# Pooled attention and a mixer in float32r pairs: low parts of the first four heads and a clamp go to GpSimd, seven more unread products, a new order

## The chip, the cores and the metric

The kernel runs on one core of one Trainium2 chip. The metric is the device time of one execution in microseconds (us); lower is better. Engines are named as in the profile: PE (TensorE, matrix products), ACT (ScalarE), DVE (VectorE), POOL (GpSimd) and SP (SyncE, which issues the DMA transfers).

## The reference

```python
# attention: B=4, H=8 heads, S=1152 keys, D=64
q_pool = q.reshape(B, H, S // 2, 2, D).mean(axis=3)          # 576 queries
scores = (1 / sqrt(D)) * q_pool @ k.transpose(0, 1, 3, 2)
attn = exp(scores - max(scores)); attn /= attn.sum(-1) + 1e-9
x = (attn @ v) as (B, 576, H * D)                            # 512 channels
# mixer: tokens, then channels; the weights are float64 words
u = x + (relu(x.T @ w_tok1) @ w_tok2).T                      # 576 -> 256 -> 576
out = u + relu(u @ w_ch1) @ w_ch2                            # 512 -> 1536 -> 512
```

## The kernel before, in words

Every matrix product runs on float32r operands, and precision is kept by splitting a float32 into a high part (rounded to float32r by a copy) and a low part (the value minus its high part). A product is then made of two or three: high by high, and the ones with a low part.

**Stage one** goes over 32 heads (4 batches of 8). A head has nine steps, each over two units of 128 keys by 288 queries. In a step PE makes the scores into a PSUM tile `s` (line 770); ACT exponentiates it twice, once as float32 into `pf` (line 780) and once rounded into `ph` (line 783); the low part `pl = pf - ph` is made by DVE or POOL (line 787); and PE multiplies `ph` and `pl` by the values `vv` into `o` (line 812). Four `pl` and five `ph` buffers go round. Beside the steps PE makes row maxima of the next head (line 706), which DVE reduces out of three PSUM banks `r` (line 708); keys and queries of the next pair of heads are turned on PE (lines 567, 590) and split; a head ends with products that turn its result (line 834), a reciprocal (line 848) and a scaled copy into `u` (line 853). The heads of `IN_PV` (0 to 3 and the odd ones from 5) get their sums of weights from an extra product; in the others DVE sums `pf` (line 794).

**The token mixer** runs after every fourth head of a half batch, first on heads 0 to 3; on PE it is placed between the products of later heads (lines 887 and 905). Its weights are loaded as 64-bit words and narrowed to float32 in `tok_weights`, in nine groups of columns, each by a chain: an absolute value on ACT (line 351), a clamp (line 352), a mask and shift (line 355), two merges (lines 358 and 361) on DVE, a high part on ACT (line 513) and a low part on DVE or POOL (line 515). Two buffers `w` go round. **Stage two**, the channel mixer (lines 1002 to 1049), follows the last head; its weights are narrowed in the same way, by DVE alone.

The order of the work is made ahead of the run by `Plan.run`: every step has an engine, a cost in ns and a due time. The planner keeps a clock for each engine and takes the step that can start first, ties going to the earlier due time. The due times are the head's start plus an offset out of the table `DUE`. A step made with `both(...)` goes to POOL or to DVE, whichever the planner's clocks let end it first, unless `on` names one. Each engine then runs its instructions in that order, with no regard to what is late on the chip.

Some products are read by nobody: `turn_over` multiplies a tile of `vv` into `o` (line 713). `WARM` of them open the program, and one follows each of the first maxima.

Of the kernel before, what the change touches and what calls it, by code (L numbers as in the profile page):

```python
# [14 lines left out]
ALU = mybir.AluOpType  # L15
# [7 lines left out]
PE, ACT, DVE, POOL, DMA, HOST = range(6)  # L23
# [11 lines left out]
    "p_lo": 0.02,  # L35
    "sum": -2.82,
    "pv": 1.78,
    "o": -107.46,
    "finish": 5.54,
    "max": -22.72,  # L40
    "max_each": 0.53,
    "prep": -32.49,
    "v": 9.58,
    "stack": 29.51,
    "stack_2": 96.51,
# [4 lines left out]
    "sum_each": 1.2,  # L50
    "pv_lo": 0.54,
    "lo_first": 7.78,
    "max_first": -120.52,
    "max_second": 37.69,
    "scores_each": -10.71,
    "p_hi": 0.84,
    "pv_one": -0.04,
    "finish_each": -14.96,
    "den_sum": -47.39,
    "x_lo": 5.05,  # L60
    "x": -54.79,
    "den": -45.22,
    "rd": -27.39,
    "u": 18.75,
    "u_each": 75.19,
    "max_of": 7.22,
    "max_row": -32.02,
    "max_first_each": -127.47,
    "q_pool": -3.78,
    "q_turn": 1.79,  # L70
    "k_each": 1.45,
    "k_hi": -42.28,
    "k_lo": 1.7,
    "q_hi": -79.72,
    "q_lo": 70.53,
    "load_kq": -48.02,
    "load_v": -163.1,
    "v_lo": -10.5,
    "load_w_tok": 117.45,
    "mix_x_lo": 3.96,  # L80
    "mix_1": 3.17,
    "mix_t": 2.11,
    "mix_2": 2.45,
    "mix_u": -79.91,
    "w_ch": 235.24,
    "w_ch_each": -64.39,
    "ut_0": -4.75,
    "ut_1": -50.96,
    "stay": 0.78,
}  # L90


# [145 lines left out]
def kernel(  # L238
# [41 lines left out]
    SP3 = S // 3  # L280
    CM = C // 2
    due = DUE
    WARM = 8
    KEEP = (0, 1, 2, 3)
    UNSTACKED = 1
    IN_PV = (0, 1, 2, 3, *range(5, 32, 2))
    CUT = 3
    FOLDS = 114
    LO = (None,) * 9
    PL = 4  # L290
    PH = 5

# [15 lines left out]
    def act_ps(n):  # L308
        return 50 + 0.833 * n
# [164 lines left out]
    def tok_weights(after):  # L474
# [19 lines left out]
        for i, c, wh, wl in (  # L494
                [(1, c, W1H[:, c], W1L[:, c]) for c in range(NQ)]
                + [(2, c, W2H[:, c], W2L[:, c]) for c in range(NJ)]):
            r = rows(c)
            words_ = (
                staged[:, c * n1:(c + 1) * n1] if i == 1 and c < 4
                else REST if i == 1 else raw[2, c])  # L500
            words_ = words_.rearrange("p (j t) -> p j t", t=2)
            n = words_.shape[1]
            for k, o in enumerate(
                    (slice(0, n),) if n <= 256 else (slice(0, n // 2), slice(n // 2, n))):
                m = o.stop - o.start
# [44 lines left out]
    def prep_kq(p, t):  # L550
# [10 lines left out]
        def keys(j):  # L561
            ps = Buf("s" if p == 0 else "r")
            o = slice(j * SP3, (j + 1) * SP3)

            def turn(ps=ps, j=j):
                for c in range(3):
                    te.transpose(
                        bank(ps)[:, c * P:(c + 1) * P],
                        KN[:, 3 * j + c].rearrange("p h d -> p (h d)"), ident)

            step(PE, 3 * TURN, turn, t + j * due["k_each"], [("kn", 0, j), ("kn", 1, j)],
                 [ps, ("kh", j), ("kl", j)], [ps])
            step(ACT, act_ps(SP3), lambda ps=ps, o=o: sc.copy(KHI[:, o], bank(ps)[:, 0:SP3]),
                 t + j * due["k_each"] + due["k_hi"], [ps], [("kh", j)])
            if p == 0:
                step(POOL, 150 + 1.1 * SP3, lambda o=o: po.tensor_copy(
                    K2[0][0:D, o], KHI[0:D, o]), t, [("kh", j)], [("k2", 0, j)])
            step(DVE, dve(SP3), lambda ps=ps, o=o: ve.tensor_sub(
                KLO[:, o], bank(ps)[:, 0:SP3], f(KHI)[:, o]),
                t + j * due["k_each"] + (due["lo_first"] if p == 0 else due["k_lo"]), [ps, ("kh", j)], [("kl", j)])  # L580
# [168 lines left out]
    def main(h, t0):  # L749
# [8 lines left out]
        for s in range(NS):  # L758
# [3 lines left out]
            for i, (fq, c) in enumerate(units):  # L762
# [23 lines left out]
            pv = h in IN_PV  # L786
            both(2 * HF, lambda e, pf=pf, ph=ph, pl=pl: e.tensor_sub(  # L787
                at(pl), pf, f(at(ph))), t + due["p_lo"], [("pf", s), ph], [pl], [pl],
                on=LO[s])
            if s in (4, NS - 1) and not pv:  # L790
                fq = s // 5
                for y in range(CUT):
# [348 lines left out]
```

## Time and profile before

| | us |
|---|---|
| median of three runs (955.95 to 961.17) | 960.82 |
| the profiled execution, whole | 961.85 |
| its span, from the first to the last instruction | 959.7 |
| PE busy in the span | 921.2 |
| DVE busy | 704.3 |
| ACT busy | 514.7 |
| POOL busy | 341.0 |

The profiled execution's own time is 2.15 us longer than its span. Busy is the time in which an engine had an instruction under way; an instruction that waits for an engine's shared resource after it has begun counts as busy.

### The profile page before, as it was taken

To read this page: it belongs to the slowest core of one execution; us is meant where nothing else is said; L and a number is where in the kernel's file an instruction comes from. 1 tells how busy PE (TensorE), PEld (TensorE's weight loads), DVE (VectorE), ACT (ScalarE), POOL (GpSimd) and SP (SyncE) were. 2 spreads that over 40 slices of the span, in tenths; PEclk is the share of its full clock that TensorE was granted. 3 is DMA by queue.
4 is the path that set the end of the run, shared out by engine and by line. 5 is a ranking of instruction groups with operands and counts; after the bars stand their busy time and mean duration, and the time that the engine had idled before them with its cause. 6 is when DMAs were issued, how large, how long until landed. Compare 5 with 4: busy or idle time off the path is not lost.

```text
span 959.7 us, 15868 instructions
## 1 busy us (share of the span) xinstructions
PE 921.2 (96%) x5850; PEld 841.8 (88%) x5850; DVE 704.3 (73%) x1277; ACT 514.7 (54%) x1040; POOL 341.0 (36%) x308
## 2 busy tenths in 40 slices
PE   6988899999999999999999999999999999999997
PEld 5767788989899898899898998989989999999996
DVE  6888999899999898999989999998882222121211
ACT  3765787776786775786767866854441111111110
POOL 1443386565483563673754844510000000000000
PEclk9978999999999999999999999999999999999999
DMA  6956537536456455365454343024430101000001
GB/s 144 257 113 146 129 79 165 128 80 155 102 128 140 97 124 131 87 155 118 99 131 114 88 99 97 24 90 132 132 110 1 66 1 33 1 33 0 30 4 33
DMA packets 89684, 91.09 MB, mean 95 GB/s; under 512 B 43852, under 2 KB 68808, under 8 KB 89608
## 3 DMA queue, kind: packets, MB, share of 16 engines
q1 hardware_dynamic: 89608, 90.09, 38.7%
q8 instruction: 46, 0.75, 0.3%
q14 instruction: 30, 0.25, 0.1%
HBM read 43.25 MB, written 4.72 MB: 50 GB/s over the span
## 4 chain that ended last, share of the span: by engine, by line
PE 63%; DVE 25%; DMA 5%; issue 3%; ACT 2%; SPq 0%; DVEq 0%; ACTq 0%
PE r L1002 14%; PE o L812 11%; PE s L1030 11%; PE s L770 9%; DVE mx L708 7%; DVE sum L794 6%; PE r L706 6%; PE r L834 3%; DVE pl L787 3%; DMA kk<-kl 2%; DMA raw<-in_moe_w_ch_dram 2%; PE o L1030 2%; PE r L905 2%; PE r L841 2%; PE r L887 1%
## 5 line engine op out<-in xcount | busy, mean ns | idle before, releaser
L787 POOL TENSOR_TENSOR pl<-pf,ph 128x576 fp32r<-128x576 f32 x182 | 260.9, 1454 | 132.1 <-ACT ph L783 93.7
L780 ACT ACTIVATE pf<-s 128x576 f32<-128x576 f32 x288 | 189.5, 662 | 90.9 <-PE s L770 84.9
L708 DVE TENSOR_REDUCE mx<-r 128x1 f32<-128x384 f32 x384 | 197.1, 548 | 15.2 <-PE r L706 12.9
L783 ACT ACTIVATE ph<-s 128x576 fp32r<-128x576 f32 x288 | 189.0, 663 | 3.8 <-PE o L812 2.8
L770 PE MATMUL s<-qq,kk 128*128 128x288 f32 x574 | 168.8, 306 | 2.2 <-ACT ph L783 1.8
L770 PE MATMUL s<-q,k 65*128 65x288 f32 x576 | 165.6, 300 | 0.0
L1010 DVE SCALAR_TENSOR_TENSOR h<-r,h 128x384 fp32r<-128x384 f32 x72 | 40.1, 557 | 169.5 <-ACT h L1008 169.4
L794 DVE TENSOR_REDUCE sum<-pf 128x96 f32<-128x864 f32 x84 | 146.1, 1752 | 0.3
L812 PE MATMUL o<-ph,vv 128*128 128x288 f32 x576 | 143.3, 304 | 1.0 <-ACT ot L817 0.9
L706 PE MATMUL r<-kk,qq 128*128 128x384 f32 x372 | 132.2, 374 | 12.6 <-DVE mx L708 6.4
L1008 ACT ACTIVATE h<-r 128x384 fp32r<-128x384 f32 x72 | 35.4, 491 | 200.3 <-PE r L1002 200.3
L812 PE MATMUL o<-pl,vv 128*128 128x288 f32 x576 | 138.7, 299 | 1.6 <-DVE pl L787 1.6
L1030 PE MATMUL s<-w,h 128*128 128x512 f32 x504 | 131.1, 394 | 0.4 <-DVE h L1010 0.4
L770 PEld LDWEIGHTS s<-qq,kk 128*128 128x128 f32 x574 | 110.0, 192 | 7.0 <-ACT ph L783 5.2
L812 PEld LDWEIGHTS o<-ph,vv 128*128 128x128 f32 x576 | 100.9, 191 | 11.4 <-ACT ot L817 3.7
L770 PEld LDWEIGHTS s<-q,k 65*128 65x128 f32 x576 | 110.6, 192 | 0.0
L1002 PE MATMUL r<-big,w 128*128 128x384 f32 x576 | 110.3, 339 | 0.3 <-DVE big L991 0.3
L1030 PEld LDWEIGHTS s<-w,h 128*128 128x128 f32 x504 | 93.4, 188 | 17.2 <-DVE h L1010 0.7
L1002 PEld LDWEIGHTS r<-big,w 128*128 128x128 f32 x576 | 102.7, 189 | 4.3 <-DVE big L991 0.5
L812 PEld LDWEIGHTS o<-pl,vv 128*128 128x128 f32 x576 | 99.6, 190 | 3.6 <-DVE pl L787 2.5
L787 DVE TENSOR_TENSOR pl<-pf,ph 128x576 fp32r<-128x576 f32 x106 | 93.6, 884 | 3.8 <-issue 1.2
L706 PEld LDWEIGHTS r<-kk,qq 128*128 128x128 f32 x372 | 71.2, 196 | 25.4 <-DVE mx L708 12.6
(135 smaller groups left out, 1258.9 us busy)
## 6 DMA issues: line engine op xcount, KB each, us to landing
raw<-in_moe_w_ch_dram SPq DMA_DIRECT2D x24, 512.0 KB, 3.8
kk<-kh SPq DMA_DIRECT2D x32, 288.0 KB, 3.3
kk<-kl SPq DMA_DIRECT2D x32, 288.0 KB
qq<-qh SPq DMA_DIRECT2D x64, 144.0 KB, 3.7
vn<-in_v_dram SPq DMA_DIRECT2D x32, 288.0 KB, 3.5
k<-kk SPq DMA_DIRECT2D x31, 288.0 KB, 5.1
kn<-in_k_dram SPq DMA_DIRECT2D x30, 288.0 KB, 4.3
qn<-in_q_dram SPq DMA_DIRECT2D x32, 256.0 KB, 3.1
```

What stands on the lines that cost most here:

```text
L706: step(PE, mm(SP3), lambda ps=ps, w=w, x=x: te.matmul(at(ps)[:, 0:SP3], w, x, start=True, stop=True), t, read, [ps], [ps])
L708: step(DVE, dve(SP3), lambda ps=ps, m=m: ve.tensor_reduce(m, at(ps)[:, 0:SP3], axis=AX.X, op=ALU.max), t + due["max_of"], [ps], [key])
L770: te.matmul(at(st)[:, i, 0:HF], w[:, c * P:(c + 1) * P], x[:, fq * HF:(fq + 1) * HF], start=(n == 0), stop=(n == len(terms) - 1))
L780: step(ACT, act_ps(2 * HF), lambda pf=pf, st=st: sc.activation(pf, at(st)[:, :, 0:HF], AF.Exp, scale=ESC), t, [(st, 0), (st, 1)], [("pf", s)])
L783: step(ACT, act_ps(2 * HF), lambda ph=ph, st=st: sc.activation(at(ph), at(st)[:, :, 0:HF], AF.Exp, scale=ESC), t + due["p_hi"], [(st, 0), ...
L787: both(2 * HF, lambda e, pf=pf, ph=ph, pl=pl: e.tensor_sub(at(pl), pf, f(at(ph))), t + due["p_lo"], [("pf", s), ph], [pl], [pl], on=LO[s])
L794: step(DVE, 65 + 1.83 * NK * HF // CUT, lambda fq=fq, cs=cs: ve.tensor_reduce(SUM[:, fq, cs], PF[:, fq * NK:(fq + 1) * NK, cs].rearrange(" ...
L812: lambda o=o, x=x, w=w, m=m, i=i, c=c, new=new, end=end: te.matmul(at(o)[0:m], w[:, c], at(x)[:, i], start=new, stop=end),
L1002: te.matmul(at(ps)[:, 0:GT], w[:, c], x[:, c], start=(c == 0 and n == 0), stop=(c == NC4 - 1 and n == 2))
L1008: step(ACT, act_ps(GT), lambda: sc.activation(at(h)[:, 0], at(ps)[:, 0:GT], AF.Relu), t, [ps], [h])
L1010: step(DVE, dve(GT), lambda: ve.scalar_tensor_tensor(out=at(h)[:, 1], in0=at(ps)[:, 0:GT], scalar=0.0, in1=f(at(h))[:, 0], op0=ALU.max, op ...
L1030: te.matmul(at(ps), a[:, x * P:(x + 1) * P], w, start=(fi == 0 and m == 0), stop=(fi == NF - 1 and m == 2))
```

## The change

It does four things. The low parts `pl` of heads 0 to 3 (`EARLY = 4`) are all made by POOL; before, the planner chose. The clamp of the token mixer's words (the second operation of `narrow`, nine times) is made by POOL and not by DVE. Seven more unread products are issued: `WARM` is 11 and not 8, and four follow the first turning of keys. And nearly all offsets in `DUE` have new values, of which two lines are shown; so the planner gives another order throughout. Lines of the changed file are 11 higher around `main`, 8 higher in `keys`, 1 higher in `narrow`.

```diff
-    "w_tok": -27.04,
-    "w_tok_each": 7.34,
+    "w_tok": 1.44,
+    "w_tok_each": 7.64,
...
-    WARM = 8
+    WARM = 11
...
-    LO = (None,) * 9
+
+    EARLY = 4
...
+                def clamp(tmp=tmp):
+                    po.tensor_scalar(
+                        out=tmp(), in0=tmp(), scalar1=F64_LEAST, scalar2=F64_MOST,
+                        op0=ALU.max, op1=ALU.min)
+
                 for n, (eng, cost, fn) in enumerate(narrow(tmp, lambda w=words_[r, o]: w, m)):
+                    if n == 1:
+                        eng, cost, fn = POOL, 150 + 1.1 * m, clamp
                     step(eng, cost, fn, t, read, [w], [w] if n == 0 else [], shared=eng == DVE)
...
             step(PE, 3 * TURN, turn, t + j * due["k_each"], [("kn", 0, j), ("kn", 1, j)],
                  [ps, ("kh", j), ("kl", j)], [ps])
+            if p == 0 and j == 0:
+                for _ in range(4):
+                    turn_over(220, t - 1, plan.steps[-1:])
...
                 at(pl), pf, f(at(ph))), t + due["p_lo"], [("pf", s), ph], [pl], [pl],
-                on=LO[s])
+                on=POOL if h < EARLY else None)
```

Counted over the whole program, DVE has 94 low parts `pl` where it had 106 (POOL 194 and not 182), no clamps of the token words where it had 9, 11 low parts of values `vv` where it had 16, 6 sums `qp` of query pairs where it had 18, 9 low parts of the mixer's input in the form 128x256 where it had 7, and 4 of the four low parts `w2l` where it had 2. By the buffers that the products read, 21 of the 36 low parts of heads 0 to 3 were DVE's before.

On PE at the start of the program (o<-vv are the unread products, s<-ident turns the first queries `qp` and keys `kn`, r<-kh,big the first maxima), before:

```order
L713 MATMUL o<-vv_122 128x512 x8
L590 MATMUL s_77<-ident,qp 128x128 x3
L567 MATMUL s_78<-ident,kn 128x128 x3
L706 MATMUL r_80<-kh,big_72 128x384
L713 MATMUL o<-vv_122 128x512
```

and now:

```order
L724 MATMUL o<-vv_122 128x512 x11
L601 MATMUL s_77<-ident,qp 128x128 x3
L575 MATMUL s_78<-ident,kn 128x128 x3
L724 MATMUL o<-vv_122 128x512 x4
L717 MATMUL r_80<-kh,big_72 128x384
```

Nothing else moved there: three products more stand ahead of the first turn, and four ahead of the first maximum.

On DVE after the keys of the second pair of heads are split (kl, ql are their low parts, w the words of the token weights, rm the maxima of the last rows), before:

```order
L787 TENSOR_TENSOR pl_163<-pf,ph_157 128x576
L787 TENSOR_TENSOR pl_164<-pf,ph_158 128x576
L614 TENSOR_TENSOR ql_120<-r_81,qh_118 128x384
L614 TENSOR_TENSOR ql_120<-r_82,qh_118 128x192
L352 TENSOR_SCALAR w_155<-w_155 128x256
L352 TENSOR_SCALAR w_156<-w_156 128x256
L355 TENSOR_SCALAR w_155<-w_155 128x256
L355 TENSOR_SCALAR w_156<-w_156 128x256
L358 SCALAR_TENSOR_TENSOR w_155<-u_66,w_155 128x256
L358 SCALAR_TENSOR_TENSOR w_156<-u_66,w_156 128x256
```

and now:

```order
L625 TENSOR_TENSOR ql_120<-r_81,qh_118 128x384
L625 TENSOR_TENSOR ql_120<-r_82,qh_118 128x192
L719 TENSOR_REDUCE rm<-r_80 128x1
L719 TENSOR_REDUCE rm<-r_81 128x1
L719 TENSOR_REDUCE rm<-r_82 128x1
L356 TENSOR_SCALAR w_155<-w_155 128x256
L359 SCALAR_TENSOR_TENSOR w_155<-u_66,w_155 128x256
L362 SCALAR_TENSOR_TENSOR w_155<-u_66,w_155 128x256
L641 TENSOR_TENSOR vv_122<-vn,vv_122 128x9x64
L523 TENSOR_TENSOR big_71<-w_155,big_70 128x256
L564 TENSOR_TENSOR qp<-qn 128x256 x2
L857 TENSOR_SCALAR den_130<-r_80 128x5
```

The low parts and the clamps are gone, and one group of words stands here where two stood side by side. Over a longer stretch: up to the reciprocal that ends head 3, DVE had 25 low parts `pl`, all 36 of its operations on token words (four for each of nine groups), 2 `w2l` and 1 `vv`; it now has 3, 17 of 27, none and 4. From there to the reciprocal of head 8 it had 11 `pl`, no words, no `w2l` and 3 `vv`; it now has 17, the other 10, all 4 and 2. From there to the reciprocal of head 31 it had 70 `pl`, 12 `vv`, 13 `qp` (6 in the form 128x256) and 3 low parts of the mixer's input in the form 128x256; it now has 74, 5, none and 5. The first product of the token mixer stands behind the end of head 6 in both orders.

On POOL from its first low part on (vv and v are the values, qp the sums of query pairs), before:

```order
L787 TENSOR_TENSOR pl_163<-pf,ph_158 128x576
L787 TENSOR_TENSOR pl_164<-pf,ph_159 128x576
L630 TENSOR_TENSOR vv_121<-vn,vv_121 128x9x64
L632 COPY v_123<-vv_121 128x9
L634 MEMSET vv_121 128x9
L787 TENSOR_TENSOR pl_162<-pf,ph_161 128x576
L556 TENSOR_TENSOR qp<-qn 128x256
L556 TENSOR_TENSOR qp<-qn 64x128
L787 TENSOR_TENSOR pl_165<-pf,ph_159 128x576
L515 TENSOR_TENSOR big_71<-w_156,big_70 128x256
```

and now:

```order
L798 TENSOR_TENSOR pl_164<-pf,ph_159 128x576
L798 TENSOR_TENSOR pl_165<-pf,ph_160 128x576
L643 COPY v_123<-vv_121 128x9
L645 MEMSET vv_121 128x9
L564 TENSOR_TENSOR qp<-qn 128x256
L564 TENSOR_TENSOR qp<-qn 64x128
L798 TENSOR_TENSOR pl_162<-pf,ph_161 128x576
L798 TENSOR_TENSOR pl_163<-pf,ph_157 128x576
L513 TENSOR_SCALAR w_155<-w_155 128x256
L798 TENSOR_TENSOR pl_164<-pf,ph_158 128x576
L798 TENSOR_TENSOR pl_165<-pf,ph_159 128x576
L798 TENSOR_TENSOR pl_162<-pf,ph_160 128x576
```

The low parts now follow one another, and the first clamp (L513) stands between two of them. From its first low part to the last of head 3 POOL has 36 low parts, 1 `vv`, 4 copies `v`, 4 clears of a column of `vv`, 7 sums `qp` (3 in the form 128x256, 4 in 64x128) and 6 clamps.

## Rows read from the trace of the kernel before

**Rows 1.** Head of the page: busy us, share of the span, instructions.

```profile
PE 921.2 (96%) x5850; PEld 841.8 (88%) x5850; DVE 704.3 (73%) x1277; ACT 514.7 (54%) x1040; POOL 341.0 (36%) x308
```

**Rows 2.** DVE's timeline: reciprocals of heads 0, 1, 3, 8 and 31.

```profile
48.81 0.19 DVE L848 RECIPROCAL rd<-den 128x5 f32<-128x5 f32 x1
84.45 0.18 DVE L848 RECIPROCAL rd<-den 128x5 f32<-128x5 f32 x1
124.14 0.18 DVE L848 RECIPROCAL rd<-den 128x5 f32<-128x5 f32 x1
218.84 0.18 DVE L848 RECIPROCAL rd<-den 128x5 f32<-128x5 f32 x1
632.59 0.18 DVE L848 RECIPROCAL rd<-den 128x5 f32<-128x5 f32 x1
```

**Rows 3.** Windows between those: length; busy us of PE, PEld, DVE, ACT, POOL; PEclk; DMA.

```profile
20.00:48.80 28.80, 24.11 (x152) 20.69 (x151) 22.74 (x49) 21.59 (x46) 12.69 (x13) 0.94 1.08 251
48.80:84.50 35.70, 29.99 (x154) 25.45 (x155) 31.75 (x63) 21.17 (x45) 16.16 (x16) 0.75 0.64 137
84.50:104.20 19.70, 17.78 (x122) 16.07 (x121) 18.05 (x37) 13.50 (x29) 7.19 (x9) 0.94 0.39 91
104.20:124.10 19.90, 17.92 (x125) 16.02 (x124) 17.19 (x35) 12.84 (x25) 5.63 (x6) 1.00 0.59 136
124.10:218.80 94.70, 91.07 (x655) 84.05 (x654) 87.97 (x145) 71.50 (x147) 67.03 (x59) 1.00 0.50 115
218.80:590.50 371.70, 363.53 (x2632) 339.72 (x2631) 348.08 (x611) 267.66 (x542) 214.75 (x185) 1.00 0.50 116
```

**Rows 4.** Windows of PE alone (busy us, granted clock, DMA), and its timeline at 55 us.

```profile
8.00:12.00 4.00, 3.13 (x10) 0.57 0.00 0
...
52.00:56.00 4.00, 2.83 (x9) 0.50 1.16 212
...
55.40 1.61 PE L706 MATMUL r<-kk,qq 128*128 128x384 f32 x3 [1.17 <-DVE mx L708]
```

**Rows 5.** Groups of 20 to 125 us: count, busy us, mean ns, idle ahead.

```profile
L787 POOL TENSOR_TENSOR pl<-pf,ph 128x576 fp32r<-128x576 f32 x16 | 24.5, 1529 | 33.1 <-ACT ph L783 26.8 <-issue 2.5 <-PE o L812 2.3
L787 DVE TENSOR_TENSOR pl<-pf,ph 128x576 fp32r<-128x576 f32 x25 | 21.1, 846 | 1.5 <-issue 1.0 <-PE o L812 0.4
```

**Rows 6.** Groups of the whole span on DVE, the forms that the change moves.

```profile
L787 DVE TENSOR_TENSOR pl<-pf,ph 128x576 fp32r<-128x576 f32 x106 | 93.6, 884 | 3.8 <-issue 1.2 <-ACT ph L783 0.7 <-PE o L812 0.4
L361 DVE SCALAR_TENSOR_TENSOR w<-u,w 128x288 uint32<-128x288 uint32 x4 | 3.9, 969 | 0.0
L352 DVE TENSOR_SCALAR w<-w 128x288 f32<-128x288 f32 x4 | 2.8, 700 | 0.1
```

**Rows 7.** Groups of the whole span on POOL.

```profile
L787 POOL TENSOR_TENSOR pl<-pf,ph 128x576 fp32r<-128x576 f32 x182 | 260.9, 1454 | 132.1 <-ACT ph L783 93.7 <-DVE mx L708 11.4 <-PE o L812 8.7
L556 POOL TENSOR_TENSOR qp<-qn 128x256 f32<-128x256 f32 x21 | 17.3, 825 | 36.9 <-PE r L590 31.8 <-DMA k<-kk 2.8 <-DMA qn<-in_q_dram 1.2
L632 POOL CAST v<-vv 128x9 fp32r<-128x9 f32 x18 | 5.7, 315 | 52.9 <-DVE vv L630 27.1 <-PE o L812 15.3 <-PE r L905 7.0
L576 POOL CAST k<-kh 64x384 fp32r<-64x384 f32 x3 | 1.5, 502 | 10.4 <-ACT kh L573 10.4
```

**Rows 8.** Timelines of DVE and POOL around 44 us.

```profile
42.95 0.29 DVE L352 TENSOR_SCALAR w<-w 128x256 f32<-128x256 f32 x1 [0.50 <-ACT w L351]
44.58 1.91 DVE L352 TENSOR_SCALAR w<-w 128x256 f32<-128x256 f32 x1
44.93 1.41 POOL L787 TENSOR_TENSOR pl<-pf,ph 128x576 fp32r<-128x576 f32 x1
```

**Rows 9.** PE's timeline at the start.

```profile
1.49 3.76 PE L713 MATMUL o<-vv 128*128 128x512 f32 x8 [1.49 <-DVE vv L435]
6.63 0.57 PE L590 MATMUL s<-ident,qp 128*128 128x128 f32 x3 [1.38 <-DVE qp L556]
8.87 0.69 PE L706 MATMUL r<-kh,big 128*128 128x384 f32 x1 [1.34 <-ACT big L599]
```

More of the change, by code (lines that the diff above doesn't have):

```diff
@@ L37 @@
     "pv": 1.78,
-    "o": -107.46,
-    "finish": 5.54,
+    "o": -98.0,
+    "finish": 7.26,
     "max": -22.72,
     "max_each": 0.53,
[L42 to L45, printed above, removed]
+    "prep": -32.61,
+    "v": 9.35,
+    "stack": 20.4,
+    "stack_2": 110.89,
     "mix": 9.83,
     "mix_x": 6.03,
-    "w_tok": -27.04,
-    "w_tok_each": 7.34,
[L50 to L54, printed above, removed]
-    "scores_each": -10.71,
[L56 to L70, printed above, removed]
-    "k_each": 1.45,
[L72 to L89, printed above, removed]
+    "w_tok": 1.44,
+    "w_tok_each": 7.64,
+    "sum_each": 1.16,
+    "pv_lo": 0.48,
+    "lo_first": 18.17,
+    "max_first": -46.26,
+    "max_second": -2.53,
+    "scores_each": -10.71,
+    "p_hi": 0.19,
+    "pv_one": 0.42,
+    "finish_each": -12.28,
+    "den_sum": -22.47,
+    "x_lo": -40.37,
+    "x": -55.82,
+    "den": -30.6,
+    "rd": -28.65,
+    "u": 91.71,
+    "u_each": 86.94,
+    "max_of": 7.03,
+    "max_row": -30.75,
+    "max_first_each": -73.07,
+    "q_pool": 3.58,
+    "q_turn": 2.24,
+    "k_each": 1.45,
+    "k_hi": -15.82,
+    "k_lo": 1.4,
+    "q_hi": -51.82,
+    "q_lo": 99.53,
+    "load_kq": -30.44,
+    "load_v": -224.43,
+    "v_lo": -10.18,
+    "load_w_tok": 153.3,
+    "mix_x_lo": 1.92,
+    "mix_1": 2.88,
+    "mix_t": 2.15,
+    "mix_2": 2.85,
+    "mix_u": -93.8,
+    "w_ch": 254.03,
+    "w_ch_each": -79.11,
+    "ut_0": -0.58,
+    "ut_1": -54.13,
+    "stay": 7.7,
 }
```

## The prediction

> **What bounds the kernel now.** I read the head of the page first, then DVE's reciprocals (one ends each head), then busy times of the engines in the windows between them, and the groups last. The page says PE 96% and DVE 73% of the span [rows 1], but DVE's share is an average over two stages. The reciprocals give the pace: head 0 is done at 48.81 us, head 1 at 84.45, head 3 at 124.14, head 8 at 218.84 and head 31 at 632.59 [rows 2]. From head 3 on that is (632.59 - 124.14) / 28 = 18.2 us a head; head 1 takes 35.6. The windows say why [rows 3]. In the later heads (218.8 to 590.5) PE is busy 363.53 of 371.7 us (98%) and DVE 348.08 (94%): both near their limit, and a gain there needs less DVE work without more for PE. In the first four heads (20 to 124.1, 104.1 us) PE is busy 24.11 + 29.99 + 17.78 + 17.92 = 89.8 us and DVE 22.74 + 31.75 + 18.05 + 17.19 = 89.7; POOL only 12.69 + 16.16 + 7.19 + 5.63 = 41.7. Head 1 is the worst of them: at a granted clock of 0.75 PE is busy 29.99 us with 154 instructions, where head 3's 125 take 17.92. The clock stood at 0.50, the lower of its two levels (1.2 GHz), from 52 to 56 us, and fell also in the window of 8 to 12 us (0.57) [rows 4]. There DVE has the token weights to narrow on top of the heads' work, and PE stands until a maximum has freed one of the three banks `r`: 1.17 us at a time at 55.40 [rows 4]. Stage two (from 632.6) is PE's alone and keeps its work.
>
> **DVE in the first four heads.** Up to head 3's reciprocal the new order takes off DVE: 22 low parts (25 to 3) at the 0.846 us that one took there [rows 5], 18.6; 9 clamps, eight at about the 0.700 of the larger form and a small one at 0.29, 5.9 [rows 6, 8]; 10 word operations that come later, about 3.3 groups of mask, merge and merge, at 0.29 (a mask is an operation of the clamp's kind) + 2 x 0.969 [rows 6, 8], 7.4; 2 `w2l`, of half a low part's columns at half its price, 0.8. It adds 3 `vv`, of a low part's shape, at 0.846: 2.5. Net -30.2: DVE's 89.7 [rows 3] become 59. POOL gets 36 low parts at 1.454, 52.3, and up to the last of them 1 `vv` (1.454), 3 sums at 0.825, 4 smaller sums (I take 0.5), 4 copies and 4 clears at the copies' 0.315, and 6 clamps [rows 7]. No row shows a clamp on POOL. From below it is bounded by the copy of nine columns, 0.315, from above by the two-input operation of 256 columns, 0.825; I take 0.502, that of the one-input cast of 384 columns on 64 partitions, which is nearest in kind [rows 7]. Together 52.3 + 1.5 + 2.5 + 2.0 + 2.5 + 3.0 = 64. PE's busy time, with head 1 at the 17.9 of heads 2 and 3, is 24.11 + 3 x 17.85 = 77.7 [rows 3]. So PE is the longest of the three (78, against 64 and 59) and, idle as little as in later heads (2%), passes head 3 at 20 + 79.4 = 99.4 us. I take 101, with 1.6 for chains between POOL and PE, against 124.1: **-23 us**. From both sides: 97.7 if PE never idles, and 113 if head 1 stays at its 29.99.
>
> That sum takes the 0.846 as freed. The Trainium skill, "SBUF — State Buffer", section "Who interferes with whom", speaks against it: GpSimd and a VectorE instruction with two SBUF inputs, or in a two-port mode, exclude each other, and the one that comes second stands until the first has ended. The trace agrees: a clamp on DVE that takes 0.29 us with POOL idle took 1.91 when POOL's low part ran from 44.93 to 46.34 [rows 8]. By that rule the 22 low parts would not leave DVE at no price; they hold the ports 1.454 and not 0.846 each [rows 5, 7].
>
> **What comes back.** The deferred work lands between heads 3 and 8, where DVE is busy 87.97 of 94.7 us (93%) [rows 3]: 10 word operations 7.4, 4 `w2l` 1.7, 6 low parts more at 0.884, 5.3 [rows 6], one `vv` less, -0.9: 13.5. At 93% DVE passes it on nearly whole: **+14 us** (low end 9, if the ten words take 0.29 each with POOL out of the way, high end 18, if each waits 0.45 longer). The token mixer doesn't wait for them: its first product stands behind head 6 in both orders. From head 8 to head 31 DVE has 4 low parts more (+3.5), 7 `vv` fewer (-6.2 at a low part's price), 13 `qp` of 256 or 128 columns fewer (-3.7 at their share of a low part's 576) and two mixer inputs of 256 columns more (+0.8): -5.6, over 94%, **-6 us** (0 if POOL's longer operations hold PE instead, -10 if the order, which now repeats every four heads, also closes half of the 8.2 us in which PE is idle there).
>
> **The seven products.** Eight took 3.76 us, 0.47 each, and PE was then idle 1.38 us until the first queries came; three more take 1.41 [rows 9]. The idle time covers them; without it they would cost that. The other four stand in the 1.34 us before the first maximum [rows 9]: at 0.47 they would be 0.5 too long, at half of that they fit. If they keep the clock up at 8 to 12 us, ten instructions busy 3.13 us [rows 4] gain at most 1.5. I take 0, between +2 and -1.5. The DMA order of the first four heads is nearly the same; transfers get no term.
>
> Sum: -23 + 14 - 6 = **-15 us**. The profiled execution took 961.85 us; 961.85 - 15 = **947 us**. (Its time is 1.0 above the median of the three runs, 960.82.) Half a per cent, 4.8 us, is about what a measurement of this kernel can tell from no change.
>
> **Rivals.**
> **It comes cheaper.** The deferred words slip into gaps that heads 3 to 8 have on DVE (7% of 94.7 is 6.7) and the steadier order gives all of its 10: -23 + 7 - 10 = -26, so 936. For it: less DVE work in sum, and an order that repeats. Against it: DVE's gaps there are short. 0.20.
>
> **The port takes it back.** From the mechanism of the 1.91 us [rows 8]: POOL is then busy 64 of some 80 us in the first four heads, against 41.7 of 104.1 before [rows 3]. DVE still has some 30 two-input or fast single-input operations there, and at 0.7 us (half of POOL's 1.454) each waits; POOL waits in its turn for DVE's. If that, some 20 us on DVE's 59 and about 12 on POOL's 64, puts POOL's chain and not PE in charge, head 3 ends at 110, and -14 + 14 - 6 leaves **-6, so 956**. The rule of the Trainium skill's "SBUF — State Buffer" above gives this time if none of its waits were covered. 0.17.
>
> **DVE stands behind the clamps: slower.** Each clamp now lies in POOL's queue between low parts, and on DVE its mask waits for it. DVE's queue is in order: behind the mask of the first group stand two merges, `vv`, `big`, `qp` and the steps that end head 0, then the maxima of head 2, for whose banks PE waits. If POOL is late by two low parts, a mask waits 2 x 1.454 = 2.9 us, nine times 26. That turns -15 into +11: **973**. It decides from 15 / 9 = 1.7 us a clamp on. For it: the order was made from planned times, and PE, once kept waiting, loses its clock as at 52 us. Against it: POOL has 16 us of slack in 80, and the values to clamp come early. 0.14.
>
> **The order does not help at all**, the later heads losing by waits between POOL and PE what the first gain: within 3 us of before, so 962. 0.07.
>
> The forecast itself, 941 to 953, has 0.42.
>
> **How the numbers follow.** The likeliest is 947. Faster than 956.0: the forecast and the cheaper case whole, and 0.45 of the port's: 0.42 + 0.20 + 0.08 = 0.70. Slower than 965.6: most of the clamps' case, 0.13. The rest, 0.17, is within. The range goes from below the cheaper case to past the one without help, 932 to 964, and leaves out the clamps' case and a little at the lower end.
>
> **What would show it.** Right: head 3's reciprocal at 97 to 105 us and head 1 in under 22; DVE in the first four heads busy some 60 us and POOL some 64; the granted clock at 1.00 from 48 to 64 us; head 8 some 9 us and head 31 some 15 us earlier than before; stage two 327 us long. Wrong: a mask (line 356) on DVE that waits for POOL by microseconds; PE idle until POOL's `pl` at line 823; POOL's low parts at 1.7 us and over; heads 3 to 8 longer than 115 us; a clock of 0.50 in heads 1 to 3.

## The result and the profile after

The changed kernel takes 943.96 us (median of 4 runs, 942.22 to 945.57); the kernel before took 961.0 beside it. The ratio is 0.9834, with a 95% interval of 0.9804 to 0.9863: faster by 17 us, and 3 us under the forecast of 947. The profiled execution of the changed kernel took 942.22 us, its span is 940.4.

The head of its page, to be laid beside [rows 1]:

```profile
PE 912.0 (97%) x5857; PEld 837.5 (89%) x5857; DVE 686.0 (73%) x1243; ACT 515.1 (55%) x1040; POOL 377.4 (40%) x342
```

Its reciprocals of heads 3, 8 and 31 (DVE's timeline, as [rows 2]):

```profile
105.05 0.19 DVE L859 RECIPROCAL rd<-den 128x5 f32<-128x5 f32 x1
...
215.73 0.18 DVE L859 RECIPROCAL rd<-den 128x5 f32<-128x5 f32 x1
...
617.04 0.19 DVE L859 RECIPROCAL rd<-den 128x5 f32<-128x5 f32 x1
```

And its windows between the reciprocals (columns as in [rows 3]), with stage two last:

```profile
20.00:45.70 25.70, 22.25 (x145) 20.05 (x146) 18.90 (x31) 20.57 (x43) 18.62 (x19) 0.93 1.07 257
45.70:69.20 23.50, 21.39 (x146) 18.62 (x145) 20.49 (x45) 15.60 (x34) 19.70 (x17) 1.00 0.87 194
69.20:86.40 17.20, 16.47 (x120) 15.09 (x119) 12.27 (x28) 13.44 (x30) 15.87 (x16) 1.00 0.45 105
86.40:105.00 18.60, 17.26 (x127) 15.92 (x127) 18.02 (x32) 13.73 (x29) 12.86 (x11) 1.00 0.50 123
105.00:215.70 110.70, 105.21 (x701) 95.07 (x700) 101.60 (x172) 80.17 (x165) 75.60 (x67) 0.94 0.52 119
215.70:576.60 360.90, 354.38 (x2605) 334.51 (x2605) 337.20 (x595) 265.10 (x532) 219.76 (x194) 1.00 0.53 116
617.00:940.40 323.40, 317.38 (x1641) 287.30 (x1640) 124.81 (x233) 70.89 (x142) 2.33 (x2) 1.00 0.15 48
```

Read in this way, head 3 ends 19.1 us earlier than before, head 8 only 3.1, head 31 15.6. It looks as if nearly all of the early gain were given back by head 8 and then won again. That is a fault of the mark. The reciprocal is one step that the order may put earlier or later against the rest. PE's count up to head 8's reciprocal shows it, in the kernel before:

```profile
0.00:218.80 218.80, 196.21 (x1259) 173.13 (x1260) 193.85 (x370) 145.48 (x301) 111.28 (x111) 0.94 0.60 137
```

and after:

```profile
0.00:215.70 215.70, 199.82 (x1301) 176.88 (x1302) 187.73 (x354) 149.64 (x310) 145.26 (x137) 0.96 0.63 145
```

After, PE has 42 more products behind it at that mark, 7 of them unread: 35 that count, and at the 363.53 / 2632 = 0.138 us of a product in the later heads [rows 3] that is 4.8 us of work done ahead. A mark that cannot move is the first exponential of a head: ACT makes nine `pf` a head, in the same sequence in every order. For heads 4, 8 and 31 (the 37th, 73rd and 280th), before:

```profile
114.28 0.68 ACT L780 ACTIVATE pf<-s 128x576 f32<-128x576 f32 x1
...
182.17 0.65 ACT L780 ACTIVATE pf<-s 128x576 f32<-128x576 f32 x1 [3.14 <-PE s L770]
...
610.35 0.65 ACT L780 ACTIVATE pf<-s 128x576 f32<-128x576 f32 x1 [0.30 <-DVE sum L794]
```

and after:

```profile
97.56 0.65 ACT L791 ACTIVATE pf<-s 128x576 f32<-128x576 f32 x1 [0.89 <-PE s L781]
...
174.38 0.65 ACT L791 ACTIVATE pf<-s 128x576 f32<-128x576 f32 x1
...
594.46 0.72 ACT L791 ACTIVATE pf<-s 128x576 f32<-128x576 f32 x1
```

By these, -16.7 us at head 4, -7.8 at head 8 (which is the 3.1 and the 4.8), -15.9 at head 31. So heads 0 to 3 gain 16.7, heads 4 to 7 give back 8.9, and heads 8 to 30 gain another 8.1. The rest of the span's 19.3 comes behind: 2.0 in head 31, 1.4 from the last exponential on. All experiments below are read by this mark.

### The profile page after: what moved, and what is told of

It reads as the page before. It is cut to its first block, busy times and chain, and to the rows that moved or that the text cites. A ratio compares the mean times of both kernels' runs of the same rounds, so it can differ in the third digit from the quotient of the medians.

```text
span 940.4 us, 15866 instructions
## 1 busy us (share of the span) xinstructions
PE 912.0 (97%) x5857; PEld 837.5 (89%) x5857; DVE 686.0 (73%) x1243; ACT 515.1 (55%) x1040; POOL 377.4 (40%) x342
## 4 chain that ended last, share of the span: by engine, by line
PE 66%; DVE 2%; ACT 1%; DMA 0%; issue 0%; POOL 0%; DVEq 0%; POOLq 0%
PE r L1013 16%; PE s L1041 12%; PE o L823 11%; PE s L781 9%; PE r L717 4%; PE o L1041 3%; PE r L916 3%; PE r L845 2%; PE r L898 2%; PE r L852 1%; PE r L1041 1%; PE r L575 1%; PE r L991 1%; DVE mx L719 1%; DVE pl L798 1%; DMA vn<-in_v_dram 0%
## 5 line engine op out<-in xcount | busy, mean ns | idle before, releaser
L798 POOL TENSOR_TENSOR pl<-pf,ph 128x576 fp32r<-128x576 f32 x194 | 278.4, 1455 | 126.3 <-ACT ph L794 76.1
L717 PE MATMUL r<-kk,qq 128*128 128x384 f32 x372 | 127.7, 362 | 11.2 <-DVE mx L719 5.2
L823 PE MATMUL o<-pl,vv 128*128 128x288 f32 x576 | 135.5, 299 | 0.5 <-DVE pl L798 0.5
L781 PEld LDWEIGHTS s<-qq,kk 128*128 128x128 f32 x574 | 109.4, 191 | 6.9 <-ACT ph L794 5.4
L1041 PEld LDWEIGHTS s<-w,h 128*128 128x128 f32 x504 | 93.4, 188 | 16.6 <-DVE h L1021 0.2
L798 DVE TENSOR_TENSOR pl<-pf,ph 128x576 fp32r<-128x576 f32 x94 | 76.6, 819 | 3.9 <-ACT ph L794 3.4
```

Source lines behind the costliest of these rows:

```text
L717: step(PE, mm(SP3), lambda ps=ps, w=w, x=x: te.matmul(at(ps)[:, 0:SP3], w, x, start=True, stop=True), t, read, [ps], [ps])
L781: te.matmul(at(st)[:, i, 0:HF], w[:, c * P:(c + 1) * P], x[:, fq * HF:(fq + 1) * HF], start=(n == 0), stop=(n == len(terms) - 1))
L798: both(2 * HF, lambda e, pf=pf, ph=ph, pl=pl: e.tensor_sub(at(pl), pf, f(at(ph))), t + due["p_lo"], [("pf", s), ph], [pl], [pl], on=POOL i ...
L823: lambda o=o, x=x, w=w, m=m, i=i, c=c, new=new, end=end: te.matmul(at(o)[0:m], w[:, c], at(x)[:, i], start=new, stop=end),
L1041: te.matmul(at(ps), a[:, x * P:(x + 1) * P], w, start=(fi == 0 and m == 0), stop=(fi == NF - 1 and m == 2))
```

## Experiments

"Order held" means that the steps are planned as in the kernel named, and only the edited instruction is issued otherwise. Ratios are to the kernel before on the same chip. "Last" is the last of the 288 exponentials; the four columns at the right add up to the span (us) of the profiled run.

Only one run of each kernel was profiled, and runs of one kernel lie up to 11.5 us apart. The profiled run took 961.85 us for the kernel before (its median in these rounds is 959.1 to 959.2) and 961.2 for the low parts planned; it took 945.89 for the new table alone, 948.76 for the table with the words early and 947.52 for the clamp's cost, each the fastest of its kernel. So the medians and the ratios say what a change is worth, and the columns say where; a difference of two or three us in one column is within this scatter.

| kernel | median (range, runs) | ratio, 95% | to head 4 | heads 4 to 7 | head 8 to last | from last on |
|---|---|---|---|---|---|---|
| before | 959.1 to 959.2 (954.6 to 966.39, 70) | 1 | 114.3 | 67.9 | 442.7 | 334.8 |
| after | 943.96 (942.22 to 945.57, 4) | 0.9834 [0.9804, 0.9863] | 97.6 | 76.8 | 432.6 | 333.4 |
| low parts back | 956.89 (948.13 to 959.67, 12) | 0.9964 [0.9937, 0.9990] | 108.4 | 78.3 | 436.3 | 334.1 |
| clamp back | 951.46 (949.59 to 953.11, 6) | 0.9923 [0.9897, 0.9949] | 106.4 | 76.5 | 435.0 | 333.4 |
| no added products | 943.66 (942.59 to 949.93, 6) | 0.9864 [0.9831, 0.9897] | 99.6 | 76.9 | 430.7 | 333.6 |
| after, old table | 955.22 (952.43 to 958.41, 12) | 0.9963 [0.9945, 0.9980] | 112.8 | 71.6 | 436.4 | 330.8 |
| products alone | 957.02 (953.12 to 959.53, 12) | 0.9972 [0.9955, 0.9989] | 109.4 | 69.7 | 442.3 | 332.8 |
| low parts alone, held | 958.75 (956.79 to 962.78, 10) | 0.9994 [0.9976, 1.0012] | 111.0 | 68.0 | 442.8 | 335.5 |
| low parts alone, planned | 955.56 (955.22 to 961.2, 10) | 0.9961 [0.9944, 0.9978] | 112.3 | 69.7 | 446.5 | 331.0 |
| new table alone | 948.98 (945.89 to 954.63, 5) | 0.9896 [0.9860, 0.9932] | 99.6 | 78.8 | 431.5 | 333.7 |
| late words alone | 959.06 (955.29 to 960.79, 12) | 0.9994 [0.9977, 1.0011] | 105.3 | 76.7 | 441.4 | 333.2 |
| table, words early | 952.39 (948.76 to 956.61, 6) | 0.9931 [0.9904, 0.9957] | 112.3 | 66.3 | 434.3 | 333.9 |
| clamp's cost as measured | 949.7 (947.52 to 952.6, 6) | 0.9903 [0.9882, 0.9924] | 101.4 | 72.9 | 437.7 | 333.7 |
| clamp planned on DVE | 942.83 (942.03 to 943.38, 4) | 0.9826 [0.9806, 0.9847] | 96.4 | 75.6 | 435.8 | 333.8 |

**Low parts back.** The changed kernel, order held; 21 of the 36 low parts of heads 0 to 3 are issued on DVE again.

```diff
-            both(2 * HF, lambda e, pf=pf, ph=ph, pl=pl: e.tensor_sub(
+            both(2 * HF, lambda e, pf=pf, ph=ph, pl=pl, d=h < 4 and
+                 "DPPDPDDPDDPPPDPDPPDPDPDDDPDPDDDDPDDD"[9 * h + s] == "D":
+                 (ve if d else e).tensor_sub(
```

> The changed kernel with its planned order held as it is, but the 21 low parts of heads 0 to 3 that were DVE's before are issued on DVE again. If DVE's relief from them makes the gain (my theory), head 3's reciprocal comes 12 to 19 us later than the changed kernel's 105 us and the whole is 8 to 18 us slower than its 944, 952 to 962. If the new order of the steps makes the gain (first rival) or the unread products with the clock (second rival), it stays within 4 us, 940 to 948.

Measured: 956.89 us, within the range expected of the relief, and the gain is nearly gone; 10.8 of the 16.6 us that the span loses are lost before head 4 (head 3's reciprocal is at 114.68, 9.6 later, less than the 12 expected). The loss isn't the same in every run and goes with the granted clock: two of the twelve took 948.13 and 948.78 at 0.992 and 0.991, the other ten 953.67 to 959.67 at 0.982 to 0.987. This order needs DVE free of the low parts. What follows is a limit too: the order was made for POOL, so the run says what the two are worth together, not what the placement is worth alone.

**Clamp back.** The changed kernel, order held; the nine clamps run on DVE.

```diff
                 def clamp(tmp=tmp):
-                    po.tensor_scalar(
+                    ve.tensor_scalar(
```

> The changed kernel with its order held, the nine clamps issued on DVE and not on POOL. The clamp took 1.06 to 1.17 us on POOL, twice what I assumed; on DVE it is 0.29 alone and up to 1.9 behind POOL. My theory, that DVE is relieved in heads 0 to 3 with room to spare: 0 to 3 us slower, 944 to 947. A rival, that the clamps on POOL hold up DVE's in-order queue: faster by 2 to 6 us, 938 to 942.

Measured: 951.46, slower than either range expected; 8.9 of the 10.9 us that the span loses are lost ahead of head 4. A large part is what meets what. In head 0 of the changed kernel a clamp of 1.05 us stands in POOL's queue ahead of three low parts, which start at 46.22 us. Here it is gone and they start at 44.41; DVE comes 1.1 us later to two sums of query pairs (44.01 against 42.88) and meets all three. DVE's timeline of this kernel, with the second of the two sums by itself below:

```profile
44.01 5.13 DVE L564 TENSOR_TENSOR qp<-qn 128x256 f32<-128x256 f32 x2
...
48.74 0.41 DVE L564 TENSOR_TENSOR qp<-qn 128x256 f32<-128x256 f32 x1
```

and POOL's and PE's:

```profile
44.41 4.12 POOL L798 TENSOR_TENSOR pl<-pf,ph 128x576 fp32r<-128x576 f32 x3
```

```profile
48.87 0.90 PE L601 MATMUL r<-ident,qp 128*128 128x128 f32 x3 [2.67 <-DVE qp L564]
```

The first sum ends just behind the third low part (44.41 + 4.12 = 48.53). In the changed kernel the pair took 1.98 us, beside one low part. PE, which turns the sums, waits 2.67 us for them, the steps that end head 0 are late, and the granted clock is 0.57 in the next 8 us, near the lower level (1.2 GHz). The window in this kernel and, under it, in the changed one:

```profile
48.00:56.00 8.00, 7.13 (x31) 6.14 (x32) 6.53 (x16) 1.46 (x3) 3.37 (x3) 0.57 1.00 241
```

```profile
48.00:56.00 8.00, 6.56 (x46) 5.81 (x45) 6.11 (x15) 3.22 (x7) 6.59 (x5) 1.00 1.03 232
```

31 products in the window instead of 46, with PE busy longer. The first exponential of head 2 comes 3.9 us later than in the changed kernel (64.71 against 60.79); the other 5.0 up to head 4 weren't followed row by row. The rule that the prediction took from the Trainium skill ("SBUF — State Buffer", section "Who interferes with whom": the second comer stands) is what these rows show, here for one DVE instruction over three of POOL's at a stretch.

**No added products.** The changed kernel, order held, the seven products not issued.

```diff
-                    turn_over(220, t - 1, plan.steps[-1:])
+                    turn_over(220, t - 1, plan.steps[-1:], issue=False)
...
-        turn_over(440, -60)
+        turn_over(440, -60, issue=i < 8)
```

> The changed kernel with its order held, the seven added unread products not issued. By the prediction (nothing for them): within 1.5 us of 944. By what the trace of the changed kernel suggests (clock at 1.00 from 8 to 12 us, the first low part on POOL at 19.96 us): the clock falls again at 8 to 12 us and the whole is 1.5 to 4 us slower, 945.5 to 948. If the clock were the chief cause, 10 us or more.

Measured: a median of 943.66, the changed kernel's time, as the prediction had it; the two ratios' intervals overlap. Two of the six runs took 949.72 and 949.93, which none of the changed kernel's four did; so few runs can't say whether the products guard against that. The first exponential comes at 20.87 us instead of 18.69, the lead of 2.1 still stands at head 8 (176.5 against 174.4), and by the last exponential it is 0.2 (607.2 against 607.0).

**After, old table.** The changed kernel with all offsets of the old table, planned anew.

```diff
-    "w_tok": 1.44,
-    "w_tok_each": 7.64,
+    "w_tok": -27.04,
+    "w_tok_each": 7.34,
...
```

> The changed kernel with the old table of due times: low parts of heads 0 to 3 and clamps on POOL, seven more products, planned anew with the offsets of before. If the low parts make the gain whatever the order, at least half of the 17 us stays, 944 to 953. If the new table makes it, 955 to 965; the old table has the token words early, so POOL's clamps and DVE's words then meet the 36 low parts in head 1.

Measured: 955.22, within what was expected if the new table makes the gain. The low parts, the clamps and the products together, planned with the old offsets, are worth 0.37%, some 3.6 us.

**Products alone.** The kernel before, order held, with the seven products.

```diff
+                if p == 0 and j == 0:
+                    for _ in range(4):
+                        te.matmul(PS_O, VV[1][:, 0], VV[1][:, 0:4], start=True, stop=True)
...
-        turn_over(440, -60)
+        turn_over(440, -60, times=4 if i == WARM - 1 else 1)
```

> The kernel before with its order held and only the seven unread products added at the same two places. By the prediction 0, between 2 slower and 1.5 faster: 958 to 961 where the kernel before takes 959 to 961. If the products pay by the clock at 8 to 12 us being full and everything then coming 2 us earlier (the first low part did, with and without them in the changed kernel): 955 to 957.

Measured: 957.02, 2.1 us faster than the kernel before beside it (959.16), at the edge of what was expected if they pay; the interval of the ratio just leaves out 1. In the profiled run the lead at the first exponential (18.67 against 20.07) isn't lost by the last (621.4 against 624.9), as it was in the new order. By these two experiments the products are worth 0 to 2 us.

**Low parts alone.** The kernel before with all low parts of heads 0 to 3 on POOL, first in the held order, then planned.

```diff
-            both(2 * HF, lambda e, pf=pf, ph=ph, pl=pl: e.tensor_sub(
+            both(2 * HF, lambda e, pf=pf, ph=ph, pl=pl, h=h: (po if h < 4 else e).tensor_sub(
```

> The kernel before with its order held, all 36 low parts of heads 0 to 3 issued on POOL. My theory (less DVE work in the first heads is the gain): 4 to 14 us faster, 946 to 956, less than in the changed kernel since the token words still fill DVE in head 1. The rival that the order makes it, and that POOL with the shared port only trades one wait for another: 957 to 966.

```diff
-                on=LO[s])
+                on=POOL if h < 4 else None)
```

> The kernel before planned anew with only EARLY = 4 added (old table, clamps on DVE, no added products). The changed kernel with the old table took 955.2 and clamps and products were worth little there if it is the table that counts: 952 to 960. If low parts on POOL were enough by themselves: 944 to 950.

Measured: 958.75 and 955.56: nothing, against the 4 to 14 us that I expected from relief of DVE, and 3.6 us. The first is the clearest look at what a low part off DVE is worth. Window of the kernel before:

```profile
20.00:125.00 105.00, 90.70 (x556) 79.14 (x556) 90.63 (x182) 69.23 (x144) 42.57 (x43) 0.89 0.70 160
```

and of the low parts alone, order held:

```profile
20.00:125.00 105.00, 93.19 (x581) 82.17 (x582) 89.15 (x163) 72.85 (x152) 73.84 (x68) 0.89 0.69 161
```

DVE (third pair) runs 19 instructions fewer and is busy only 1.5 us less, POOL (fifth) is busy 31 us more, and PE is 25 products ahead, some 3.4 us, which agrees with the 3.3 at head 4. The clock is 0.89 in both. Nine masks and eight merges of 288 columns, as many in both windows, take 18.5 us there instead of 11.2. Where the place of the other DVE work isn't changed, it stands behind POOL for much of what the low parts leave.

**New table alone.** The kernel before with the new offsets and nothing else, planned.

```diff
-    "w_tok": -27.04,
+    "w_tok": 1.44,
...
```

> The kernel before with only the new table: the planner chooses the engine of every low part again, clamps on DVE, no added products. My theory (DVE relieved by moving low parts): little, 952 to 961. The rival that the order by itself makes the gain, by the token words coming later: 942 to 949.

Measured: 948.98, with runs from 945.89 to 954.63: by the ratios 10 of the 16 us, at the edge of what was expected if the order by itself makes the gain. All three parts are there without a low part or a clamp that was told to move: -14.6 to head 4, +10.9, -11.2. And the planner moved hardly any: of the first 36 low parts 20 are DVE's, where 21 were. Windows from 20 us to head 4's first exponential, in the kernel before, with the new table alone, and in the changed kernel:

```profile
20.00:114.30 94.30, 80.85 (x485) 69.84 (x485) 82.19 (x165) 62.23 (x131) 39.24 (x40) 0.87 0.71 162
```

```profile
20.00:99.60 79.60, 72.95 (x484) 64.79 (x485) 70.62 (x143) 58.14 (x122) 41.26 (x40) 0.96 0.80 191
```

```profile
20.00:97.60 77.60, 71.31 (x486) 64.11 (x487) 62.41 (x126) 57.23 (x121) 63.42 (x57) 0.98 0.77 181
```

The table alone gives PE nearly all that the whole change gives it there: the clock at 0.96 instead of 0.87, and 6.7 us of idle time instead of 13.5. The 8.2 us that the change takes off DVE beyond that go with 2.0 us of time. What the change is worth beyond the table, some 6 us by the ratios, is by elimination the low parts' move planned with it, since leaving out the products, or planning the clamps on DVE, changes nothing that can be told. A kernel with the table and that move alone wasn't run.

**Late words alone, and the table without them.** Of the new table only the offsets that move the token words; then all the others.

```diff
-    "w_tok": -27.04,
-    "w_tok_each": 7.34,
+    "w_tok": 1.44,
+    "w_tok_each": 7.64,
...
-    "load_w_tok": 117.45,
+    "load_w_tok": 153.3,
```

> The kernel before with only the three offsets of the token words from the new table (w_tok, w_tok_each, load_w_tok), planned anew: 24 of DVE's 36 word operations stand ahead of head 3's end and not all 36; the low parts stay as they were (23 on DVE there). The new table alone took 949. If the late words make that gain (what I now think, against my prediction's low parts): 945 to 953. If it is the rest of the table: 956 to 963.

```diff
-    "o": -107.46,
-    "finish": 5.54,
+    "o": -98.0,
+    "finish": 7.26,
...
-    "max_first": -120.52,
-    "max_second": 37.69,
+    "max_first": -46.26,
+    "max_second": -2.53,
...
```

> The kernel before with the new table but these three offsets of the words as they were: all 36 word operations ahead of head 3's end again, 18 low parts on DVE there. If the late words make the table's gain: 955 to 964. If the rest of the table does: 946 to 952.

Measured: 959.06 and 952.39: the late words don't make the table's gain, as I had come to think (945 to 953), and the other offsets make most of it (a median just past the 946 to 952 expected of that case). The two halves of the table do different things. Late words win 9.0 us to head 4 and give 8.8 back by head 8: a loan. The other offsets change little there (-2.0 and -1.6) and win 8.4 from head 8 on, in the fastest of their six runs. Together the two win more ahead of head 4 (14.6) than each by itself (9.0 and 2.0).

**The clamp's cost and its place, planned.** In the changed kernel the planner takes 150 + 1.1 m ns for a clamp of m columns on POOL, 0.43 us at 256; the trace has 1.07. One kernel gives it the measured cost, one leaves the clamp on DVE, with all else as changed.

```diff
-                        eng, cost, fn = POOL, 150 + 1.1 * m, clamp
+                        eng, cost, fn = POOL, 200 + 3.35 * m, clamp
```

> The changed kernel with the clamp's cost on POOL given to the planner as the trace showed it (200 + 3.35 ns a column, 1.06 us for 256, where it has 150 + 1.1), all else the same. If a planned order that knows how long POOL is held by a clamp matters: 936 to 942. If not, or if the offsets fit only the costs that they were made with: 943 to 950.

```diff
-                    if n == 1:
-                        eng, cost, fn = POOL, 150 + 1.1 * m, clamp
```

> The changed kernel without the clamp's move: the planner puts the nine clamps on DVE and orders all anew (new table, EARLY = 4, seven products). With the order held they cost 7.5 us on DVE, by one wait for POOL in head 0. If that was an accident of the held order: 941 to 948. If the clamps on DVE cost by themselves what the prediction took (5.9 us of DVE time): 948 to 954.

Measured: 949.7 and 942.83. The true cost makes it slower, 0.9903 against 0.9834, and not where the clamps are: head 8's first exponential comes at 174.3 and 174.4 us, and the 5.1 us are lost behind it, where the other order gives DVE 5.4 us more work up to head 31. It looks as if the offsets fit the costs that they were made with; how they were made is not on record. Without the clamp's move the kernel is as fast as with it. No version beats the changed kernel by more than can be told.

## Why the prediction was right, step by step

**The sum.** Forecast -15 us; -17 by the medians, -19.3 between the two profiled spans. The terms were -23, +14 and -6, set at reciprocals, where they came out as -19.1, +16.0 and -12.5; by the fixed mark as -16.7, +8.9 and -8.1, with -3.4 behind that no term had. The first two erred against each other; their sum, -9 at head 8, was -7.8. That the total is within 3 us while the terms miss by 2 to 6 is in part luck.

**The first term: PE's busy time as forecast, its idle time too small.** PE is busy 22.25 + 21.39 + 16.47 + 17.26 = 77.4 us up to head 3's reciprocal (forecast 77.7). What was mis-sized is its idle time: 2% and 1.6 us for chains, 3.3 in all, where 85.0 - 77.4 = 7.6 were measured. So the reciprocal came at 105.05 and not at 101, at the edge of the 97 to 105 given. PE's longest wait there is for keys by DMA, 2.2 us (2.3 before); none of its idle times there is put down to a low part, so that sign of being wrong did not come, nor did a clock of 0.50 in heads 1 to 3.

**Relief of DVE in the first four heads: right in kind, a third too large, and worth less than I took it for.** I took 30.2 us off DVE's 89.7 and expected 59; the windows give 18.90 + 20.49 + 12.27 + 18.02 = 69.7. The step that failed is "takes the 0.846 as freed", and the clamps with it: DVE's low parts fell by 18.2 us and its clamps by 5.9, as counted (18.6 and 5.9), but what stayed grew longer. In the sum this cost nothing, since PE was the longest of the three at 78. The larger fault is to take DVE's low parts for what holds up these heads: with the new table alone 20 of them stay, and head 4 begins 2.0 us behind the changed kernel. The masks show best what grew. Those of the kernel before (L355), in groups of the whole span on DVE:

```profile
L355 DVE TENSOR_SCALAR w<-w 128x256 uint32<-128x256 uint32 x4 | 1.6, 421 | 0.0
L355 DVE TENSOR_SCALAR w<-w 128x288 uint32<-128x288 uint32 x4 | 1.2, 297 | 0.0
L355 DVE TENSOR_SCALAR w<-w 64x256 uint32<-64x256 uint32 x1 | 0.3, 291 | 0.0
```

and masks (L356) and merges of the changed kernel:

```profile
L359 DVE SCALAR_TENSOR_TENSOR w<-u,w 128x256 uint32<-128x256 uint32 x4 | 4.0, 998 | 0.0
L362 DVE SCALAR_TENSOR_TENSOR w<-u,w 128x256 uint32<-128x256 uint32 x4 | 3.5, 869 | 0.0
L356 DVE TENSOR_SCALAR w<-w 128x288 uint32<-128x288 uint32 x4 | 3.3, 826 | 0.0
...
L356 DVE TENSOR_SCALAR w<-w 64x256 uint32<-64x256 uint32 x1 | 2.9, 2872 | 0.0
L356 DVE TENSOR_SCALAR w<-w 128x256 uint32<-128x256 uint32 x4 | 2.8, 709 | 0.0
```

The nine masks take 9.0 us. Before they took 3.1, and the nine clamps that are gone 5.9. All the word operations on DVE sum to 23.3 us in 27 instructions; before, to 23.2 in 36. The mask now stands where the clamp stood. One on DVE's timeline:

```profile
56.54 1.37 DVE L356 TENSOR_SCALAR w<-w 128x256 uint32<-128x256 uint32 x1
```

and on POOL's:

```profile
56.33 1.43 POOL L798 TENSOR_TENSOR pl<-pf,ph 128x576 fp32r<-128x576 f32 x1 [1.74 <-issue]
57.72 1.11 POOL L513 TENSOR_SCALAR w<-w 128x256 f32<-128x256 f32 x1
```

The mask began 0.21 us after POOL's low part and ended 0.15 behind it; with POOL out of the way one took 0.28 (at 65.85 us), and the longest took 2.87. A mask that waits for POOL by microseconds was named as a sign of being wrong; it came in some of the nine. With the clamps planned on DVE all 36 word operations take 24.0 us there, against the 23.3 of 27, which agrees with that kernel being as fast. The same happened before the change: in [rows 8] the clamp began at 44.58, before the low part at 44.93, but beside two sums of POOL's that ran from 43.18 to 44.97, and it stood through the low part too.

**POOL** was put at 64 us and is busy 18.62 + 19.70 + 15.87 + 12.86 = 67.1; six clamps at 1.06 to 1.17 instead of 0.502 are 3.6 of that. Head 1 took 23.5 us and not under 22, at a granted clock of 1.00, as forecast for 48 to 64 us.

**What comes back: right, and shown by the late words alone** (-9.0, then +8.8). I had +14 for all that is deferred; by the fixed mark it cost 8.9. The place where it lands is head 4. DVE's timeline there:

```profile
113.05 1.62 DVE L523 TENSOR_TENSOR w2l<-w,w2h 128x288 fp32r<-128x288 f32 x1
114.60 1.72 DVE L805 TENSOR_REDUCE sum<-pf 128x96 f32<-128x864 f32 x1
116.26 0.99 DVE L719 TENSOR_REDUCE mx<-r 128x1 f32<-128x384 f32 x2
117.19 1.69 DVE L805 TENSOR_REDUCE sum<-pf 128x96 f32<-128x864 f32 x1
...
119.74 1.61 DVE L805 TENSOR_REDUCE sum<-pf 128x96 f32<-128x864 f32 x1
121.28 1.00 DVE L719 TENSOR_REDUCE mx<-r 128x1 f32<-128x384 f32 x2
```

PE's timeline and window:

```profile
119.40 1.15 PE L717 MATMUL r<-kk,qq 128*128 128x384 f32 x2 [0.86 <-DVE mx L719]
121.87 0.69 PE L717 MATMUL r<-kk,qq 128*128 128x384 f32 x1 [1.32 <-DVE mx L719]
```

```profile
120.00:124.00 4.00, 2.68 (x10) 2.28 (x10) 4.00 (x6) 1.64 (x3) 3.94 (x6) 0.50 0.27 74
```

DVE has no gap from 113.05 to 123 us; its sums (head 4 has them, heads 0 to 3 don't) and a word's low part of 1.62 us hold up the maxima, PE waits 0.86 and 1.32 us for banks, and from 120 to 124 us its clock is at the lower level (0.50). It looks like head 1's stall of before [rows 4], moved and made shorter. The prediction had the deferred work pass on "nearly whole", but named no such place.

**Heads 8 to 31: right sign, a little small.** Forecast -6, measured -8.1. The counts were right, a price was not. DVE's groups from head 8's reciprocal to head 28's, before (218.8 to 590.5 us):

```profile
L787 DVE TENSOR_TENSOR pl<-pf,ph 128x576 fp32r<-128x576 f32 x59 | 53.5, 907 | 1.5 <-ACT ph L783 0.4
...
L630 DVE TENSOR_TENSOR vv<-vn,vv 128x576 fp32r<-128x576 f32 x11 | 8.8, 797 | 0.5 <-ACT vv L627 0.2
...
L556 DVE TENSOR_TENSOR qp<-qn 128x256 f32<-128x256 f32 x6 | 2.5, 420 | 0.0
L556 DVE TENSOR_TENSOR qp<-qn 64x128 f32<-64x128 f32 x7 | 1.9, 274 | 0.0
```

and after (215.7 to 576.6):

```profile
L798 DVE TENSOR_TENSOR pl<-pf,ph 128x576 fp32r<-128x576 f32 x62 | 51.0, 825 | 1.8 <-ACT ph L794 1.6
...
L641 DVE TENSOR_TENSOR vv<-vn,vv 128x576 fp32r<-128x576 f32 x5 | 3.8, 754 | 0.1
```

The values and sums that left come to 5.0 and 4.4 us (6.2 and 3.7 were counted, up to head 31). But the low parts, which I had add 3.5, cost 2.5 less: each takes 0.825 instead of 0.907. Of 59 before, 11 took over 0.9 us, 1.55 on average, and the others 0.760; of 62 after, 7, at 1.40, and the others 0.750. The traces say why: each of these 18 began while an instruction of POOL's ran and ended 0.61 or 0.62 us behind that one's end.

DVE's busy time falls from 348.08 to 337.20 us at the same share (94 and 93%), and the window from 371.7 to 360.9: the step "DVE near its limit, so its work is time" held. By the fixed mark, from head 8 to head 31, DVE is busy 399.9 of 428.2 us before, 399.1 of 426.8 with the late words alone, 395.5 of 425.2 with the clamp's cost, 392.1 of 421.8 with the words early and 390.1 of 420.1 after: the stretch follows DVE's work through all five. The new table alone has a price of 0.832 there, with the words early 0.834, the late words alone 0.876, and the old table with the rest of the change 0.920; so the price goes with the offsets, and more with those that don't move the words. Which of these place the steps so that they meet POOL less often, the runs don't say.

**The seven products**: forecast 0, between +2 and -1.5. Left out of the new order they change the time by nothing that can be told; added to the old they gave 2.1. The first exponential came 1.4 us earlier than before. How it is lost again in the later heads was not followed up.

**Stage two** was put at an unchanged 327 and is 323.4 from the reciprocal on. Behind the reciprocal stand 7 products fewer (1641 and 1648), so part of that is the mark again; from the last exponential on it is 1.4 shorter.

**The rivals.** "It comes cheaper" (936) had one thing right, by the fixed mark the deferred work costs less than 14; but the first heads gained less. "The port takes it back" (956) is the mechanism behind the lost third, and it fits what the low parts alone show in the old order (958.75); it did not decide: PE's busy time stayed above DVE's and POOL's in the first four heads (77.4 against 69.7 and 67.1), in the later heads DVE's low parts stand behind POOL less often (7 of 62, 11 of 59 before), and POOL's low parts are not stretched (1.471 us in the first four heads, 1.529 before [rows 5]). "DVE stands behind the clamps" (973) did not come: a mask is longer by 0.65 us on average, under the 1.7 from which it would have decided. What the prediction did not weigh is that the offsets by themselves, with as many low parts on DVE as before, bring 10 of the 16 us.

## What to carry to other kernels

Measure progress by work that every order does in the same sequence (the n-th exponential, a count of products), not by a step that the order may move. Where two engines make each other wait, as DVE and POOL did here, taking an operation off one of them frees its time only where nothing else then stands in its place: price the neighbours as well, nine masks here took 9.0 us where masks and clamps together had taken 9.0. And ask first whether the relieved engine is the one that the others wait for: here the first heads gained nearly as much with 20 low parts still on it. Deferring work out of a crowded start is a loan if the place it goes to is as full. Where a change is a placement and a new table of offsets, try each with and without the other before saying which of them pays.

## What the runs showed of the hardware that was not expected

The clamp, a one-input operation with two constants, is dear on POOL. Groups of the changed kernel:

```profile
L564 POOL TENSOR_TENSOR qp<-qn 128x256 f32<-128x256 f32 x27 | 20.3, 754 | 47.9 <-PE r L601 42.6 <-DMA k<-kk 5.2
...
L513 POOL TENSOR_SCALAR w<-w 128x288 f32<-128x288 f32 x4 | 4.7, 1167 | 4.8 <-ACT w L352 4.8
L513 POOL TENSOR_SCALAR w<-w 128x256 f32<-128x256 f32 x4 | 4.3, 1072 | 0.7 <-ACT w L352 0.7
```

1.072 us for 256 columns, over the 0.754 of a two-input sum of the same shape (the prediction took that row, then 0.825, as its bound from above), twice the 0.502 that I chose, and 3.7 times the 0.29 of DVE with POOL idle [rows 8]. And one DVE instruction can stand through several of POOL's: with the clamps back on DVE one sum stood from 44.01 until three low parts had ended at 48.53, where such a sum takes 0.42 on average in the later heads of the kernel before. The bounds of a price from near rows are bounds only for operations of the same kind.
